# Values' lone product last, PSUM pools swapped by halves, gates from the exponential, and three loads of the setup at other tiles

## The chip, the core and the metric

The kernel runs on one core of one Trainium2 chip. A core has a matmul engine (PE, TensorE), VectorE (DVE), ScalarE (ACT), GpSimd (POOL) and SyncE (SP). SP issues nearly all transfers of this kernel, in the order of the program: an issue that waits holds up all issues behind it. The metric is the device time of one execution in microseconds (us), the median over several runs. The profile is one execution, taken by the hardware profiler; its span runs from the first to the last instruction.

## What is computed

Two attention layers over the same 2048 tokens of width 512, with 32 heads of 16, mixed by a gate per token. Layer A is full softmax attention. Layer B is causal attention inside each of four segments of 512 tokens, plus a memory that is carried from segment to segment. All arithmetic is float32 (matmuls work on sums of two fp32r parts, so one product of two float32 matrices is three products of parts).

```python
g = _sigmoid((x * gate_w).sum(-1, keepdims=True))
a = _A_ref(x, A_wqkv, A_wo)                    # full attention
b = _B_ref(x, B_wq, B_wk, B_wv, B_wo, B_beta)  # four segments, with memory
return g * a + (1 - g) * b
# inside B, per segment:
    g = _sigmoid(beta); num = phi(q) @ M; den = phi(q) @ z + 1e-6
    o = g * (num / den) + (1.0 - g) * a_dot
    M = M + phi(k).T @ v;  z = z + phi(k).sum()
```

## The kernel before, in words

The kernel has two parts. In the **main part** (from about 289 us to the end) PE computes scores and weighted values, ACT the exponentials, DVE the row maxima. The change has no instruction there. In the **setup** (the first 289 us) the projections are made, and everything is stored to DRAM scratch (`qdB`, `kdB`, `kdA`, `vdA`, `vdB`), from where the main part loads it.

The setup is written out in *slots* of twelve matmuls of 512 columns, counted in `now[0]`. Each slot has four *places*, one after each three matmuls, and a function that is posted to (slot, place) issues its instructions there (`post` counts from the present slot, `post_at` is absolute). So each engine's order is fixed by these numbers. The stretches that matter:

- Slots 0 to 21: values and queries of the first half of the tokens. Slots 22 to 35: keys of A.
- **Slots 36 to 49: `v_pair` for the second half of the tokens**, called twice, for row blocks 0, 1 and then 2, 3. Each call makes seven products (a Strassen-like scheme, `ORDER`), one slot each: p1, p2, p7, p6, p5, p3, p4. Two sums X and Y per block live in PSUM: p1, p6, p5 and p3 add to X, whose partial results ACT copies out (`copy_x`); p2 is a Y of its own ("the lone product"), and p7 starts a second Y that p4 ends. DVE adds a copied X and a Y into the values `vs` after p2 (L548), p5 (L553) and p4 (L557). PSUM pools `pr`, `me` and `sm` have 2, 2 and 4 banks; a tile of a pool waits until the tile that had its bank is read. X is taken from `pr`, Y from `me`, in both calls.
- **Slots 50 to 81 (S0 = 50), called tiles 0 to 31 below**: for each of four token chunks c, four query tiles (8c to 8c+3) and four key tiles (8c+4 to 8c+7) of layer B, by `qk_tile`. A tile's PSUM result is copied by ACT (`full`, L426), rounded by ACT to its high part (`q1`, L427), its low part is made by DVE (`q2`, L434), and SP stores both (L423). `q1` and `q2` have three buffers each, so a tile needs the stores of the tile three before. For most tiles POOL makes min(x, 0) (`mn`), ACT its exponential (`ex`, one buffer, L440) and DVE phi (`ph`, L445). At tiles 13, 21 and 29 `mem_q` multiplies by the memory (`num`, `den`) and stores `numd` and `dend` to DRAM; `mem_k` transposes phi(k) (`tps`) and adds to the memory (`mps`), with values loaded back from `vdB` (`load_vB`).
- Beside these, row maxima for layer A (`some_max`, PE L242 into a `sm` bank, DVE reduction L275) run four at a time from slot 39 on.
- **Loads of the setup**: `staged` loads a weight or an x chunk (1 MB in four transfers) and splits it into two parts at given slots; `load_gate` loads four row blocks of x (1 MB) at tiles 2, 8, 16 and 21, and three and four tiles later DVE multiplies them by `gate_w` and sums (`gate_logit`, L781) into `glog`. The product goes to a scratch tile `jk` with the tag `dn`, a single buffer that it shares with the `dn` tile of `mem_q`. `load_vB` loads 2 x 544 KB at tiles 1, 11 and 19.
- **The gates**: `betas` (slot 29) makes sigmoid(beta); `gates` (tile 28) transposes `glog`, takes the sigmoid on ACT, and stores g and 1 - g through POOL. ACT holds one set of function tables at a time: Sigmoid and Exp here are in different ones, so each of them is preceded by an ACT_TABLE_LOAD where the other was last. `gates` ends with an Exp of one number that brings the exponential's tables back.

Of the kernel before, what the change touches and what calls it, by code (L numbers as in the profile page):

```python
# [10 lines left out]
F32 = mybir.dt.float32  # L11
F32R = mybir.dt.float32r
AF = mybir.ActivationFunctionType
ALU = mybir.AluOpType
# [5 lines left out]
D = 512  # L20
# [27 lines left out]
def gated_mix(ctx, tc, x, xT, wqkv, a_wo, b_wq, b_wk, b_wv, b_wo, beta, gate_w, out):  # L48
# [284 lines left out]
    with ExitStack() as p0:  # L333
# [180 lines left out]
                    post(0, 1 + 2 * g, lambda p=p, g=g: done(p, g))  # L514
                slot(prods, not first)

        def v_pair(xo, cs, bs, fill=None, tags=("full", "full", "am", "am")):
# [24 lines left out]

            def done(p, b):
                n = bs.index(b)
                if p == "p1":
                    t["1", b] = copy_x(b, tags[n])
                elif p == "p2":
                    to_vs(p, b, lambda o: V.tensor_add(o, view(Y[b]), view(t["1", b])))  # L548
                elif p == "p6":
                    t["a", b] = copy_x(b, ("q1", "q1", "q1", "q2")[n] if len(bs) == 4 else "am")  # L550
                elif p == "p5":
                    t["5", b] = copy_x(b, tags[n])
# [5 lines left out]
            xbanks = [sm_bank] * 4 if len(bs) == 4 else [pr_bank] * 2  # L558
            ybanks = [pr_bank, pr_bank, me_bank, me_bank] if len(bs) == 4 else [me_bank] * 2
            for p, x, w in ORDER:  # L560
                x, w = xo[x], vops[w]
                if fill and p == "p7":
                    fill()
                prods = []
                for b, xb, yb in zip(bs, xbanks, ybanks):
                    if p == "p1":
                        X[b] = xb()
                    elif p in ("p2", "p7"):
                        Y[b] = yb()
                first = p in ("p1", "p2", "p7")  # L570
                outer = fill and p in ("p1", "p2")
                order = [(b, 0, a, c) for a, c in ((0, 0), (0, 1), (1, 0)) for b in bs] + \
                    [(b, 1, a, c) for b in bs for a, c in PARTS] if outer else \
                    [(b, k, a, c) for b in bs for k in range(2) for a, c in PARTS]
                left = {b: 6 for b in bs}
                for i in range(0, len(order), 12):
                    part = order[i:i + 12]
                    prods = []
                    for m, (b, k, a, c) in enumerate(part):
                        ps = X[b] if p in ("p1", "p6", "p5", "p3") else Y[b]  # L580
                        left[b] -= 1
                        prods.append((ps, x[a][k][:, b * 128:(b + 1) * 128], w[c][k], first and left[b] == 5, left[b] == 0))
                        if left[b] == 0:
                            post(0, m // 3, lambda p=p, b=b: done(p, b))
                    slot(prods, not first)
# [134 lines left out]
        def staged(src, to, key, raws_, homes, load, splits, eng):  # L720

            r = []

            def load_():
                r.extend(raws_())
                load4(src, r)

            def split_(k):
                if k == 0:
                    to[key] = [h if isinstance(h, list) else unit4(h) for h in homes]  # L730
                split(to[key][0][k], to[key][1][k], r[k], eng)
            post_at(*load, load_)
            for k in range(KT):
                post_at(*splits[k], lambda k=k: split_(k))

        def at_u(i):
            return lambda: unit4(i, F32)
# [5 lines left out]
        staged(b_wk, wB, "k", at_u(4), (9, 5), (45, 0), [(48 + k, 3) for k in range(KT)], P)  # L743
        staged(xchunk(1), xcs, 1, at_u(8), (6, 10), (47, 0), [(53 + k, 2) for k in range(KT)], V)
        staged(xchunk(2), xcs, 2, at_u(2), (3, 4), (S0 + 4, 0), [(S0 + 9 + k, 2) for k in range(KT)], V)
        staged(xchunk(3), xcs, 3, at_u(2), (10, 8), (S0 + 14, 0), [(S0 + 18 + k, 2) for k in range(KT)], V)
        vB = {}

        def load_vB(c):
            vB[c] = [vp.tile([128, NG, 2, 4, 17], F32, tag="vs", name="vs") for _ in range(2)]  # L750
            for i, t in enumerate(vB[c]):
                nc.sync.dma_start(t.rearrange("p g b h e -> p g (b h e)"),
                                  vdB[c][:, :, 2 * i:2 * i + 2].rearrange("p g b e -> p g (b e)"))
        for c, n in ((0, 1), (1, 11), (2, 19)):
            post_at(S0 + n, 1, lambda c=c: load_vB(c))

        gw = {}
# [12 lines left out]
                    raw(t)[64 * r + 48:64 * r + 50], ones.unsqueeze(1).broadcast_to([2, 2, CH])))  # L770

        def betas():
            nc.scalar.activation(gh, gh, AF.Sigmoid)
            nc.vector.tensor_scalar(ogh, gh, -1.0, 1.0, op0=ALU.mult, op1=ALU.add)
            for o in range(NO):
                nc.vector.tensor_scalar_mul(gmask[:, o], bmask, gh[:, o:o + 1])
        post_at(29, 0, betas)

        def gate_logit(xg, col):
            jk = wk1.tile([128, D], F32, tag="dn", name="jk")  # L780
            nc.vector.scalar_tensor_tensor(jk, xg, 1.0, gw[0], op0=ALU.mult, op1=ALU.mult,  # L781
                                           accum_out=glog[:, col:col + 1])

        def load_gate(c):
            t = unit4((3, 7, 6, 6)[c], F32)
            for b in range(4):
                t0 = c * CH + 128 * b
                nc.sync.dma_start(t[b], x[t0:t0 + 128])
            for b in range(4):
                post(3 + b // 2, 1 + 2 * (b % 2), lambda b=b: gate_logit(t[b], 4 * c + b))  # L790
# [95 lines left out]
        for n in range(36, S0):  # L886
# [15 lines left out]
        def gates():  # L902
            gps = me_ps.tile([128, CH], F32, tag="me", name="gps")
            nc.tensor.transpose(gps[:16, :128], glog, identf)
            gt = wk1.tile([128, 4, 128], F32, tag="gw", name="gt")
            nc.scalar.activation(gt[:16, 0], gps[:16, :128], AF.Sigmoid)

            nc.scalar.activation(gt[:1, 2, 0:1], eps[:1], AF.Exp)
            nc.vector.tensor_scalar(gt[:16, 1], gt[:16, 0], -1.0, 1.0, op0=ALU.mult, op1=ALU.add)
            for i in range(2):  # L910
                nc.gpsimd.dma_start(gd[i].rearrange("(b t) -> b t", t=128), gt[:16, i])

        for c in range(NCH):
            post_at(S0 + (2, 8, 16, 21)[c], 2, lambda c=c: load_gate(c))
        post_at(S0 + 28, 0, gates)
        for c in range(NCH):
            for o in range(NO):
                qk_tile(wB["q"], xcs[c], o, qd["B", o, c], pqs.append if c else None)
            for o in range(NO):
                then = (lambda pk, o=o, c=c: beside_max(lambda: mem_k(o, c, pk, vB[c]))) if c + 1 < NCH else None  # L920
                qk_tile(wB["k"], xcs[c], o, kd["B", o, c], then)
# [503 lines left out]
```

## Time and profile before

| what | value |
|---|---|
| median of 3 runs | 1760.22 us (1756.73 to 1760.93) |
| the profiled execution | 1755.57 us, its span 1753.4 us |
| granted TensorE clock, mean | 0.999 |
| DVE, ACT, POOL busy | 1605.4, 1445.7, 695.1 us |
| ACT_TABLE_LOADs in the first 300 us | 5, of 1.28 us each |

How to read it: the profile's page gives busy time by engine. A timeline row gives the start, the duration, the engine, the source line, what is written from what, its shape and count, and in brackets the idle time of the engine before it and what ended that. "SPq" rows are the issues of transfers, not the transfers. A row of stretches gives, for each from:to, its length, PE's busy time with the count of matmuls, the granted clock as a share, the mean busy share of the 16 DMA engines, and what they moved. The source lines are those of the kernel before; in the changed one those behind `gate_logit` are one higher.

### The profile page before, as it was taken

How to read it: one execution, taken by the hardware profiler on the slowest of the kernel's cores; microseconds unless marked ns; L12 is line 12 of the kernel's file. 1: busy time of each engine (PE TensorE's matmuls, PEld its weight loads, DVE VectorE, ACT ScalarE, POOL GpSimd, SP SyncE). 2: the span in 40 equal slices, each digit the busy share in tenths (PEclk: the TensorE clock that was granted, in tenths of full speed). 3: DMA queues.
4: the chain of work that ended last, by engine and by line, in shares of the span. 5: the costliest groups of instructions: out<-in, count | busy, mean ns of one | idle time of the engine just before them, and what ended most of it. 6: DMA issues, size and time to landing. Idle time of an engine off the chain costs nothing.

```text
span 1753.4 us, 41543 instructions
## 1 busy us (share of the span) xinstructions
PE 1736.4 (99%) x15157; PEld 878.6 (50%) x15157; DVE 1605.4 (92%) x3371; ACT 1445.7 (82%) x2779; POOL 695.1 (40%) x944
## 2 busy tenths in 40 slices
PE   9999999999999999999999999999999999999998
PEld 7876665444444444444444444444444444444444
DVE  7767867999999999999999999999999999999931
ACT  6543657889898898888898888889889889889884
POOL 1011434324262518353435353444444353535443
PEclk9999999999999999999999999999999999999999
DMA  7677876434454446454545454444444444544542
GB/s 247 197 252 208 286 254 204 120 97 145 119 146 110 136 135 184 127 151 122 142 136 142 130 142 134 135 136 130 148 120 147 127 138 116 152 120 144 149 154 62
DMA packets 167987, 264.96 MB, mean 151 GB/s; under 512 B 38936, under 2 KB 79928, under 8 KB 167784
## 3 DMA queue, kind: packets, MB, share of 16 engines
q1 hardware_dynamic: 166840, 261.07, 50.3%
q8 instruction: 120, 1.97, 0.5%
q0 software_dynamic: 800, 0.97, 0.3%
q14 instruction: 83, 0.68, 0.1%
q10 hardware_dynamic: 144, 0.26, 0.1%
HBM read 177.74 MB, written 83.25 MB: 149 GB/s over the span
## 4 chain that ended last, share of the span: by engine, by line
PE 93%; DVE 3%; DMA 2%; ACT 1%; issue 1%; SPq 0%; DVEq 0%; ACTq 0%
PE ops L155 40%; PE st L1061 27%; PE sm L242 14%; PE pr L385 7%; PE pair L385 2%; PE sm L155 2%; DVE pm L275 1%; DMA qdB<-q 1%; DMA u<-xT 0%; DVE u L403 0%; DVE ph L445 0%; DVE q L434 0%; PE mt_ps L232 0%; PE sm L1061 0%; DVE jk L781 0%
## 5 line engine op out<-in xcount | busy, mean ns | idle before, releaser
L1084 ACT ACTIVATE p<-st 128x512 f32<-128x512 f32 x2261 | 1191.6, 601 | 145.9 <-PE sm L242 93.6
L275 DVE TENSOR_REDUCE pm<-sm 128x1 f32<-128x512 f32 x2048 | 1279.4, 690 | 13.8 <-PE sm L242 13.1
L242 PE MATMUL sm<-kA,qA 48*128 48x512 f32 x2048 | 663.7, 424 | 0.5
L1061 PE MATMUL st<-qA,kA 50*128 50x512 f32 x2014 | 656.7, 432 | 0.0
L155 PE MATMUL ops<-p,vA 128*17 128x256 f32 (+3 forms) x6360 | 552.2, 445 | 0.0
L1061 PEld LDWEIGHTS st<-qA,kA 50*128 50x128 f32 x2014 | 326.8, 185 | 423.5 <-ACT p L1084 380.4
L242 PEld LDWEIGHTS sm<-kA,qA 48*128 48x128 f32 x2048 | 338.4, 185 | 13.0 <-issue 4.2
L1185 POOL TENSOR_TENSOR rcp<-rec,minus 128x32 f32<-128x32 f32 x43 | 234.9, 5463 | 80.8 <-DMA rec<-dend 76.0
L290 DVE CUSTOM_DVE_ANT_0 rest<-sm,mask 128x128 f32<-128x128 f32 (+3 forms) x512 | 249.7, 488 | 0.0
L155 PEld LDWEIGHTS ops<-p,vA 128*17 128x17 f32 x6360 | 129.2, 96 | 214.7 <-issue 183.6
L1065 POOL TENSOR_SCALAR_AFFINE_SELECT p<-p 128x512 f32<-128x512 f32 x128 | 79.8, 640 | 266.5 <-ACT p L1084 262.1
L242 PE MATMUL sm<-kB,qB 48*128 48x128 f32 (+3 forms) x512 | 166.1, 384 | 0.0
L385 PE MATMUL pr<-u,u 128*128 128x512 f32 x392 | 103.4, 403 | 6.1 <-ACT full L426 5.0
L1061 PE MATMUL st<-qB,kB 50*128 50x512 f32 (+1 forms) x495 | 105.4, 329 | 0.3 <-ACT mt L235 0.3
L1061 PEld LDWEIGHTS st<-qB,kB 50*128 50x128 f32 x495 | 68.6, 186 | 62.3 <-ACT p L1084 50.4
L155 PE MATMUL ops<-p,vB 128*17 128x128 f32 (+3 forms) x1504 | 88.3, 350 | 0.2 <-ACT part L1275 0.2
L385 PEld LDWEIGHTS pr<-u,u 128*128 128x128 f32 x392 | 72.7, 191 | 27.2 <-ACT full L426 6.6
L242 PEld LDWEIGHTS sm<-kB,qB 48*128 48x128 f32 x512 | 79.9, 184 | 0.0
L214 POOL TENSOR_TENSOR dm<-pm 128x32 f32<-128x32 f32 x32 | 7.9, 246 | 166.5 <-DVE pm L275 166.5
L431 POOL TENSOR_SCALAR mn<-full 128x512 f32<-128x512 f32 x24 | 37.8, 1577 | 71.2 <-ACT full L426 71.2
L223 POOL CAST ms<-pm 128x16 fp32r<-128x16 f32 x32 | 6.3, 198 | 127.2 <-DVE pm L290 127.1
L1201 POOL TENSOR_TENSOR v<-v,inv 128x512 f32<-128x512 f32 x31 | 39.9, 1286 | 29.3 <-DMA inv<-rdA 22.2
(224 smaller groups left out, 1419.3 us busy)
## 6 DMA issues: line engine op xcount, KB each, us to landing
kA<-kdA SPq DMA_DIRECT2D x256, 128.0 KB
vA<-vdA SPq DMA_DIRECT2D x31, 544.0 KB
kA<-kdA SPq DMA_DIRECT2D x256, 64.0 KB
qB<-qdB SPq DMA_DIRECT2D x192, 64.0 KB
kB<-kdB SPq DMA_DIRECT2D x192, 64.0 KB
kdA<-q SPq DMA_DIRECT2D x32, 256.0 KB
qA<-qdA SPq DMA_DIRECT2D x64, 128.0 KB
qdB<-q SPq DMA_DIRECT2D x32, 256.0 KB
```

Of the source, the lines that this page charges most:

```text
L155: behind[0] = nc.tensor.matmul(*args, **kw)
L214: nc.gpsimd.tensor_sub(dm, pm[:, :, :, 2:4], pm[:, :, :, 0:2])
L242: nc.tensor.matmul(ps[:, n0:n0 + n], rows(qt[u][:, :, s * 128:(s + 1) * 128], h, 48), rows(k[:, :, k0:k0 + n], h, 48), start=True, stop=True)
L275: nc.vector.tensor_reduce(pm[:, h, s, kc:kc + 1], ps, axis=AX.X, op=ALU.max, negate=True)
L290: nc.vector.tensor_tensor_reduce(out=tri["rest"][:, 0:w], in0=ps[:, n0:n0 + w], in1=tri["mask"][:, CH - w:], scale=-1.0, scalar=3.0e38, op ...
L385: nc.tensor.matmul(ps, l, r, start=start, stop=stop, skip_group_check=chained)
L431: nc.gpsimd.tensor_scalar_min(ph["mn"], full, 0.0)
L1061: nc.tensor.matmul(ps[:, n0:n0 + CH - q0], rows(k[:, :, b * 128:(b + 1) * 128], h, 50), rows(q[:, :, q0:], h, 50), start=True, stop=True)
L1065: nc.gpsimd.affine_select(out=x, in_=x, pattern=[[0, 4], [1, 128]], base=0, channel_multiplier=-1, compare_op=ALU.is_ge, fill=0.0)
L1084: nc.scalar.activation(p[:, h], ps, AF.Exp, scale=SCALE)
L1185: eng.tensor_tensor(r, rec, minus, op=ALU.pow)
L1201: eng.tensor_mul(k["v"], k["v"], k["inv"])
```

## The change

Three parts.

1. `v_pair` in slots 36 to 49 makes p2 last (p1, p7, p6, p5, p3, p4, p2). Its Y is taken from the pool of X. The first call has X in `me` and Y in `pr`, the second the reverse. Copies of p6 go to the tag `q1`, those of p5 to `am`. The first two query tiles take their bank from `me`.
2. Both sigmoids become Exp of -x on ACT, then add 1 and reciprocal on DVE; the Exp of one number is gone. `betas` moves from slot 29 to slot 17, `gates` from tile 28, place 0 to tile 25, place 1.
3. `load_gate` runs at tiles 2, 8, 13 and 18, `load_vB` for c = 2 at tile 21, and the last x chunk at tile 15 (its splits at 19 to 22); `gate_logit` writes its product over x itself, so `jk` is gone. The buffers `u0` to `u10` are dealt out anew to suit.

```diff
-            for p, x, w in ORDER:
+            xbanks = [xbank] * 2 if xbank else [sm_bank] * 4
+            ybanks = [ybank] * 2 if ybank else [pr_bank, pr_bank, me_bank, me_bank]
+            for p, x, w in ORDER if fill else ORDER[:1] + ORDER[2:] + ORDER[1:2]:
...
-                        Y[b] = yb()
+                        Y[b] = yb() if fill or p == "p7" else xb()
...
-        staged(xchunk(3), xcs, 3, at_u(2), (10, 8), (S0 + 14, 0), [(S0 + 18 + k, 2) for k in range(KT)], V)
+        staged(xchunk(3), xcs, 3, at_u(2), (9, 5), (S0 + 15, 0), [(S0 + 19 + k, 2) for k in range(KT)], V)
...
-        for c, n in ((0, 1), (1, 11), (2, 19)):
+        for c, n in ((0, 1), (1, 11), (2, 21)):
...
-            nc.scalar.activation(gh, gh, AF.Sigmoid)
+            nc.scalar.activation(gh, gh, AF.Exp, scale=-1.0)
+            nc.vector.tensor_scalar_add(gh, gh, 1.0)
+            nc.vector.reciprocal(gh, gh)
...
-        post_at(29, 0, betas)
+        post_at(17, 0, betas)
...
-            jk = wk1.tile([128, D], F32, tag="dn", name="jk")
-            nc.vector.scalar_tensor_tensor(jk, xg, 1.0, gw[0], op0=ALU.mult, op1=ALU.mult,
+            nc.vector.scalar_tensor_tensor(xg, xg, 1.0, gw[0], op0=ALU.mult, op1=ALU.mult,
...
-            t = unit4((3, 7, 6, 6)[c], F32)
+            t = unit4((4, 7, 5, 3)[c], F32)
...
-        v_pair(xo1, (2, 3), range(2), tags=("full", "full"))
-        v_pair(xo1, (2, 3), range(2, 4), tags=("full", "full"))
+        v_pair(xo1, (2, 3), range(2), xbank=me_bank, ybank=pr_bank)
+        v_pair(xo1, (2, 3), range(2, 4), xbank=pr_bank, ybank=me_bank)
...
-            nc.scalar.activation(gt[:16, 0], gps[:16, :128], AF.Sigmoid)
-
-            nc.scalar.activation(gt[:1, 2, 0:1], eps[:1], AF.Exp)
+            nc.scalar.activation(gt[:16, 0], gps[:16, :128], AF.Exp, scale=-1.0)
+            nc.vector.tensor_scalar_add(gt[:16, 0], gt[:16, 0], 1.0)
+            nc.vector.reciprocal(gt[:16, 0], gt[:16, 0])
...
-            post_at(S0 + (2, 8, 16, 21)[c], 2, lambda c=c: load_gate(c))
-        post_at(S0 + 28, 0, gates)
+            post_at(S0 + (2, 8, 13, 18)[c], 2, lambda c=c: load_gate(c))
+        post_at(S0 + 25, 1, gates)
...
-                qk_tile(wB["q"], xcs[c], o, qd["B", o, c], pqs.append if c else None)
+                qk_tile(wB["q"], xcs[c], o, qd["B", o, c], pqs.append if c else None, bank=me_bank if c == 0 and o < 2 else None)
```

The order on PE at the start of the second `v_pair` call. `u_252` is block 2 of the left operand of p1 and `u_253` that of p2, `u_256` with `qtmp` is p7, and `sm` rows are the maxima. Before:

```order
L242 MATMUL sm<-kA_192,qA_1220 128x512 x4
L385 MATMUL pr<-u_252,u_906 128x512 x12
L242 MATMUL sm<-kA_193,qA_1220 128x512 x4
L385 MATMUL pr<-u_253,u_938 128x512 x12
L242 MATMUL sm<-kA_193,qA_1220 128x512 x4
L385 MATMUL pr<-u_256,qtmp 128x512 x12
```

Now the same place:

```order
L385 MATMUL pr<-u_253,u_946 128x512 x12
L242 MATMUL sm<-kA_192,qA_1222 128x512 x4
L385 MATMUL pr<-u_252,u_914 128x512 x12
L242 MATMUL sm<-kA_193,qA_1222 128x512 x4
L385 MATMUL pr<-u_256,qtmp 128x512 x12
```

p7 no longer follows p2 of its own call: the p2 that stands ahead of p1 here is the last product of the first call.

The order on SP from the stores of tile 18 to those of tile 22 (`qdB` and `kdB` rows are the stores, two per tile; `vs<-vdB` is the load of values, `u<-x` the gate's x, `numd` and `dend` the memory's results). Before:

```order
L174 DMA kB_200<-kdB_92 16x2x512 x6
L423 DMA qdB_111<-q_2589 128x512
L752 DMA vs<-vdB_126 128x8x136 x2
L769 DMA kB_201<-qtmp 2x2x512
L423 DMA qdB_111<-q_2590 128x512
L769 DMA kB_201<-qtmp 2x2x512
L423 DMA qdB_119<-q_2661 128x512
L423 DMA qdB_119<-q_2662 128x512
L423 DMA kdB_96<-q_2697 128x512
L423 DMA kdB_96<-q_2698 128x512
L788 DMA u_2720<-x 128x512 x4
L830 DMA numd_130<-u_2753 128x512 x4
```

Now, from the last store of tile 17 (between the two pieces stand the other rows of `kA` and those of `qB` and `kB`, as before):

```order
L423 DMA qdB_103<-q_2516 128x512
L789 DMA u_2540<-x 128x512 x4
L769 DMA kB_200<-qtmp 2x2x512
L177 DMA kA_198<-kdA_64 32x1024
L177 DMA kA_198<-kdA_64 16x1024
```

```order
L423 DMA qdB_111<-q_2588 128x512
L769 DMA kB_201<-qtmp 2x2x512
L423 DMA qdB_111<-q_2589 128x512
L769 DMA kB_201<-qtmp 2x2x512
L423 DMA qdB_119<-q_2654 128x512
L423 DMA qdB_119<-q_2655 128x512
L423 DMA kdB_96<-q_2686 128x512
L752 DMA vs<-vdB_126 128x8x136 x2
L423 DMA kdB_96<-q_2687 128x512
L831 DMA numd_130<-u_2742 128x512 x4
```

The gate's x moved from behind the stores of tile 20 to ahead of the loads of `kA`, `qB` and `kB`; the values moved from between the stores of tile 18 to between those of tile 20, and `numd` follows them with one store between.

The order on ACT around the gates (`gt` is the gate, `gps` the transposed logits). Before:

```order
L427 CAST q_3014<-full 128x512
L440 ACTIVATE ex<-mn 128x512
L906 ACT_TABLE_LOAD
L906 ACTIVATE gt<-gps 16x128
L908 ACT_TABLE_LOAD
L908 ACTIVATE gt<-eps 1x1
L426 COPY full<-pr 128x512
```

Now:

```order
L427 CAST q_2884<-full 128x512
L907 ACTIVATE gt<-gps 16x128
L849 COPY pt<-tps 128x512
L440 ACTIVATE ex<-mn 128x512
L426 COPY full<-pr 128x512
```

The gate's activation stands three tiles earlier and alone. On ACT's whole list one ACT_TABLE_LOAD is left of five, the one ahead of the first copy.

More of the change, by code (lines that the diff above doesn't have):

```diff
@@ L515, in k_pair, with v_pair @@
                 slot(prods, not first)
-        def v_pair(xo, cs, bs, fill=None, tags=("full", "full", "am", "am")):
+        def v_pair(xo, cs, bs, fill=None, xbank=None, ybank=None):
             X, Y, t, vs = {}, {}, {}, {}
@@ L545, in done @@
                 if p == "p1":
-                    t["1", b] = copy_x(b, tags[n])
+                    t["1", b] = copy_x(b, ("full", "full", "am", "am")[n])
                 elif p == "p2":
@@ L549, in done @@
                 elif p == "p6":
-                    t["a", b] = copy_x(b, ("q1", "q1", "q1", "q2")[n] if len(bs) == 4 else "am")
+                    t["a", b] = copy_x(b, ("q1", "q1", "q1", "q2")[n])
                 elif p == "p5":
-                    t["5", b] = copy_x(b, tags[n])
+                    t["5", b] = copy_x(b, ("full", "full", "am", "am")[n] if fill else "am")
                     to_vs(p, b, lambda o: V.tensor_add(o, view(Y[b]), view(t["5", b])))
@@ L557, in done @@
                     to_vs(p, b, lambda o: V.tensor_add(o, view(Y[b]), view(t["a", b])))
-            xbanks = [sm_bank] * 4 if len(bs) == 4 else [pr_bank] * 2
-            ybanks = [pr_bank, pr_bank, me_bank, me_bank] if len(bs) == 4 else [me_bank] * 2
-            for p, x, w in ORDER:
+            xbanks = [xbank] * 2 if xbank else [sm_bank] * 4
+            ybanks = [ybank] * 2 if ybank else [pr_bank, pr_bank, me_bank, me_bank]
+            for p, x, w in ORDER if fill else ORDER[:1] + ORDER[2:] + ORDER[1:2]:
                 x, w = xo[x], vops[w]
@@ L742, in gated_mix @@
         staged(xchunk(0), xcs, 0, raw_ph, (K4[3], 7), (40, 1), spread(48), V)
-        staged(b_wk, wB, "k", at_u(4), (9, 5), (45, 0), [(48 + k, 3) for k in range(KT)], P)
-        staged(xchunk(1), xcs, 1, at_u(8), (6, 10), (47, 0), [(53 + k, 2) for k in range(KT)], V)
-        staged(xchunk(2), xcs, 2, at_u(2), (3, 4), (S0 + 4, 0), [(S0 + 9 + k, 2) for k in range(KT)], V)
-        staged(xchunk(3), xcs, 3, at_u(2), (10, 8), (S0 + 14, 0), [(S0 + 18 + k, 2) for k in range(KT)], V)
+        staged(b_wk, wB, "k", at_u(4), (10, 8), (45, 0), [(48 + k, 3) for k in range(KT)], P)
+        staged(xchunk(1), xcs, 1, at_u(2), (9, 3), (47, 0), [(53 + k, 2) for k in range(KT)], V)
+        staged(xchunk(2), xcs, 2, at_u(5), (6, 4), (S0 + 4, 0), [(S0 + 9 + k, 2) for k in range(KT)], V)
+        staged(xchunk(3), xcs, 3, at_u(2), (9, 5), (S0 + 15, 0), [(S0 + 19 + k, 2) for k in range(KT)], V)
         vB = {}
```

## The prediction

> **What bounds the kernel now.** I read the page's first two lines, then PE's busy time by stretches, cut where stages of the setup begin.
>
> ```profile
> span 1753.4 us, 41543 instructions
> PE 1736.4 (99%) x15157; PEld 878.6 (50%) x15157; DVE 1605.4 (92%) x3371; ACT 1445.7 (82%) x2779; POOL 695.1 (40%) x944
> ```
>
> ```profile
> 104.00:156.71 52.71, 50.18 (x222) 1.00 0.74 223
> 156.71:210.43 53.72, 52.10 (x378) 1.00 0.86 269
> 210.43:242.05 31.62, 31.62 (x298) 1.00 0.70 224
> 242.05:282.31 40.26, 34.49 (x298) 0.96 0.67 230
> 282.31:1753.40 1471.09, 1466.00 (x13534) 1.00 0.47 135
> ```
>
> PE is busy 99% and sets the end; all its idle time is 17 us. The rows are slots 36 to 49 with some of what precedes them, tiles 0 to 13, 14 to 21, 22 to 29, and the rest. The change has no instruction in the last row, where PE is full, so what the setup gains should reach the end whole. The third and fourth row hold the same work (298 matmuls each, eight tiles), and take 31.62 and 40.26: **the fourth loses 8.64 us**, of which PE shows 5.77 as idle; the rest is slower matmuls.
>
> Next, PE's own rows, in time order, at its waits:
>
> ```profile
> 107.08 5.75 PE L385 MATMUL pr<-u,u 128*128 128x512 f32 x24 [1.10 <-DVE full L500]
> ...
> 140.03 1.63 PE L385 MATMUL pr<-u,qtmp 128*128 128x512 f32 x6 [1.43 <-DVE vs L548]
> ...
> 159.66 1.98 PE L242 MATMUL sm<-kA,qA 48*128 48x512 f32 x4
> ...
> 245.00 0.73 PE L242 MATMUL sm<-kA,qA 48*128 48x512 f32 x4
> ...
> 251.86 2.29 PE L242 MATMUL sm<-kA,qA 48*128 48x512 f32 x4
> ...
> 255.45 4.61 PE L385 MATMUL pr<-u,u 128*128 128x512 f32 x12 [0.48 <-ACT full L426]
> ...
> 262.91 3.00 PE L385 MATMUL pr<-u,u 128*128 128x512 f32 x12 [0.48 <-ACT full L426]
> ...
> 277.26 3.03 PE L385 MATMUL pr<-u,u 128*128 128x512 f32 x12 [2.62 <-ACT full L426]
> ```
>
> Two waits in `v_pair` (1.10 and 1.43). Maxima that take 2.29 in place of 0.73. A tile that takes 4.61 in place of 3.00. And 2.62 at tile 29. What stands behind those of tiles 24 to 29 is on DVE, ACT and SP:
>
> ```profile
> 250.52 0.69 DVE L434 TENSOR_TENSOR q<-full,q 128x512 fp32r<-128x512 f32 x1 [6.07 <-DMA qdB<-q]
> ...
> 260.35 0.69 DVE L781 SCALAR_TENSOR_TENSOR jk<-u,gw 128x512 f32<-128x512 f32 x1 [5.55 <-DMA dend<-dn]
> ```
>
> ```profile
> 273.67 1.28 ACT L906 ACT_TABLE_LOAD   x1
> 274.96 0.27 ACT L906 ACTIVATE gt<-gps 16x128 f32<-16x128 f32 x1
> 275.25 1.28 ACT L908 ACT_TABLE_LOAD   x1
> ...
> 276.65 0.56 ACT L426 COPY full<-pr 128x512 f32<-128x512 f32 x1
> ```
>
> ```profile
> 224.64 2.02 SPq L788 DMA_DIRECT2D u<-x  x4
> ...
> 233.34 2.87 SPq L177 DMA_DIRECT2D kA<-kdA  x4
> ...
> 241.90 0.36 SPq L423 DMA_DIRECT2D qdB<-q  x1
> 242.31 1.35 SPq L752 DMA_DIRECT2D vs<-vdB  x2
> 243.70 0.69 SPq L769 DMA_DIRECT2D kB<-qtmp  x1
> 244.49 0.33 SPq L423 DMA_DIRECT2D qdB<-q  x1
> ...
> 249.79 1.76 SPq L788 DMA_DIRECT2D u<-x  x4
> 251.66 2.71 SPq L830 DMA_DIRECT2D numd<-u  x4
> ```
>
> SP runs some 10 us behind. It issues the loads of kA, qB and kB from 233.34 to 241.9. So the second store of tile 18 goes out only at 244.49, behind 1.1 MB of values. Tile 21's low part needs its buffer, and DVE stands for 6.07. Then x and `numd` follow at once, `dend` behind them, and `jk`, sharing a buffer with `dn`, stands for 5.55. Bytes moved in the 20 us before 242, and in the 20 us behind:
>
> ```profile
> DMA packets 2362, 4.13 MB, mean 207 GB/s; under 512 B 436, under 2 KB 468, under 8 KB 2358
> ...
> DMA packets 4987, 6.33 MB, mean 316 GB/s; under 512 B 404, under 2 KB 2452, under 8 KB 4985
> ```
>
> **Part 1, values.** With X of the first call in `me`, p1 no longer waits for DVE's last add of the keys (in `pr`): 1.10 goes. p7 now takes it one product (2.7 us) later, after those adds have ended. In the second call p7 wants a Y bank one product after the first call's p2, no longer straight behind its own p2, whose add ends late:
>
> ```profile
> 139.21 0.68 DVE L548 TENSOR_TENSOR vs<-pr,vt 128x512 f32<-128x512 f32 x1
> ...
> 157.34 1.36 DVE L403 TENSOR_TENSOR u<-ph,kA 128x512 fp32r<-128x512 f32 x1
> 158.62 2.47 DVE L275 TENSOR_REDUCE pm<-sm 128x1 f32<-128x512 f32 x4
> ```
>
> So 1.43 goes too. What is late next is DVE: the splits of the x chunk (0.6 to 1.36 each) stand in slots 48 and 49, and the maxima at 159.66 already wait 1.98 - 0.73 = 1.25 for it. A slot is 3.6 us (3.00 and 0.73, which overlap a little); DVE has 2.47 of maxima, 0.6 per add or split. Slots 47 to 49 now ask 3.7, 3.7, 4.9 = 1.5 too much; with p2 last, slots 48 and 49 ask 4.9 each, 2.6 too much. The wait may grow by up to 1.1; I take 0.6. **Values: -1.10 - 1.43 + 0.6 = -1.9** (bounds -2.5 and -1.4).
>
> **Part 2, gates.** Two table loads and two activations keep ACT from 273.67 to 276.65, 2.98 us, and PE waits 2.62 for the copy behind them. With Exp alone one activation of 0.27 stays, at a tile where ACT waits anyway. DVE gets an add and a reciprocal. The nearest row of a reciprocal is
>
> ```profile
> 1736.58 0.35 DVE L1181 RECIPROCAL rec<-rec 128x32 f32<-128x32 f32 x1 [4.30 <-DMA rec<-odA]
> ```
>
> 0.35 for 32 columns; 128 columns lie between that and four times it, 1.4. I take 0.8, hidden by PE's two banks per pool; uncovered, it costs that. POOL's store of the gates holds up `mn` of the next tile about as long. `betas` moves eight small operations (some 1 us of DVE) to slot 17, where DVE runs without a gap up to this row:
>
> ```profile
> 70.97 0.43 DVE L403 TENSOR_TENSOR kA<-u,kA 128x256 fp32r<-128x256 f32 x1 [2.00 <-ACT kA L402]
> ```
>
> The 2.00 of slack takes them; without it, 1 us. The other two table loads lie where PE does not wait: nothing. The Trainium skill (ScalarE: Activation LUTs, "What ACT_TABLE_LOAD costs") adds a drain of 1.38 us to each switch; by it the gates would give back 2.8 us more, but the activation at 274.96 begins where the load ends, so the rows show no drain.
>
> **Part 3, loads.** The gate's x goes out before the kA block, in the stretch of 207 GB/s, and takes the SP time that the load at 224.64 (2.02) leaves free; so the stores of tile 18 go out at about 243 to 244, as now, but with nothing large ahead. I take 2 us to land (the slot of 6.07 minus 1.1 MB at 316 GB/s, 3.5, gives 2.6), so DVE's 6.07 shrinks to about 2, which two banks of `pr` absorb. The 5.55 of `jk` cannot recur: there is no `jk`, and x has landed. What is late next: values and `numd`, 2.1 MB, now stand together ahead of tile 21's stores, 6.7 us at 316 GB/s, from about 246 to 253. Tile 24 wants those buffers at about 253. I leave 1.0 of PE's loss for it. **Tiles 22 to 29: -8.64 + 1.0 = -7.6**, gates included (bounds -8.6, and -1.7 below).
>
> In tiles 12 to 17 SP issues as many loads as now, x at 13 and the chunk at 15 for the chunk at 14 and x at 16. But the chunk now stands ahead of tile 14's stores. DVE has gaps there that take up some of a delay, such as this one:
>
> ```profile
> 227.13 0.69 DVE L445 SCALAR_TENSOR_TENSOR ph<-full,ex 128x512 f32<-128x512 f32 x1 [1.16 <-ACT ex L440]
> ```
>
> I take **+0.5** (0 to 6.0, what such a queue costs now at tiles 22 to 27: 8.64 - 2.62).
>
> Sum: -1.9 - 7.6 + 0.5 = **-9.0**. Against the profiled execution, 1755.57 (span 1753.4 and 2.2 around it), that is 1746.6. The median of the runs shown is 1760.22, 4.6 above it, and I forecast on its scale: 1751.
>
> **Rivals.**
> - *The wait stays where it is.* Values and `numd` together delay the stores as values and x do now, and tiles 22 to 27 keep their 6.0. For it: the same bytes go in the same 20 us but for 1 MB. Against: nothing waits for `dend`. Then the gates alone give 2.62, less 1.0 that the next `num` products wait when PE comes early: -1.6. With values -1.9: -3.5, 1756.7. Chance 0.20.
> - *The queue moves to tiles 14 to 17.* Half of 6.0 arises there: -9.0 + 2.5 = -6.5, 1753.7. Chance 0.12.
> - *Slower:* the same mechanism at full price in both places. The chunk ahead of tile 14's stores costs 6.0 and tiles 22 to 27 keep 6.0: -3.5 + 6.0 = +2.5, 1762.7. It decides when stores cost PE more than 6.0 + 3.5 = 9.5 us in tiles 12 to 27. Against: the third row has no idle PE now. Chance 0.05.
> - *DVE bounds slots 46 to 50*, so that the bank swap does not do what it says and the values give nothing: -7.1, 1753.1. Chance 0.08.
> - *The half clock stays.* These rows bear on it:
>
> ```profile
> 252.10:255.50 3.40, 2.42 (x9) 1.00 1.04 348
> 255.50:258.90 3.40, 3.40 (x9) 0.53 0.99 379
> ...
> 272.60:276.00 3.40, 2.04 (x9) 1.00 0.28 102
> ```
>
>   The 4.61 (1.6 more than 3.00) is the granted clock at half for one stretch, behind 3.4 us with PE at 71%. At 272.6 PE is at 60% and keeps its clock. If the fall does not hang on the wait, it stays: -7.4, 1752.8. The Trainium skill (TensorE: Matmul & The Clock Gate, "What's actually happening") lets the clock fall after an idle window of about 3.4 us; the length agrees with the 3.4 us at 0.53, but no such idle stretch precedes it here, and by that rule the wait would not be its cause. I keep the wait as cause. Chance 0.08.
>
> **How the numbers follow.** The forecast has the rest, 0.47. About 0.3% (5.3 us) is what a measurement can tell from no change. Faster by more: the forecast, the half clock, DVE and most of the moved queue, 0.71. Slower by more: 0.03, the slower rival beyond its price. Same: 0.26. The range: at best all of 8.6 and 2.5 go (-11.1, 1749), and the runs shown reach 3.5 below their median: 1745. Above, the first rival gives 1756.7 and two of three runs lie within 0.7 of 1760: 1759.
>
> **What would show it.** Right: p1 at slot 36 and p7 at slot 45 without a wait; `gate_logit` never waiting for `dend`; no table load behind the first; the stretch of tiles 22 to 29 near 32.6 us, at full clock. Wrong: DVE waits of several us for `qdB` or `kdB` stores at tiles 16 to 27, maxima of slot 50 above 2.6 us, or a main part that is longer by what the setup gains.

## The result, and the profile after

| kernel | median, us | runs | ratio to the kernel before, 95% interval |
|---|---|---|---|
| changed kernel | 1745.63 (1744.79 to 1747.14) | 4 | 0.9924, 0.9907 to 0.9942 |
| the same on a second chip | 1746.47 (1745.55 to 1748.38) | 4 | 0.9932, 0.9916 to 0.9947 |

The kernel before had 1759.38 beside the first row and 1758.14 beside the second, so the change is worth 13.75 and 11.7 us. The forecast, 1751.0, was 9.2 below the median it started from; the range (1745 to 1759) holds the result at its low end. The two profiled executions differ by less, 1755.57 against 1745.41, since the profiled run of before was among its fastest (24 runs of it on a third chip went from 1754.4 to 1759.3). Stage lengths below are from the profiled pair, in which the span shrank by 9.7.

The page's head after the change:

```profile
span 1743.7 us, 41524 instructions
...
PE 1732.8 (99%) x15157; PEld 878.0 (50%) x15157; DVE 1606.5 (92%) x3375; ACT 1439.4 (83%) x2774; POOL 694.2 (40%) x944
```

PE's busy time by stretches, from the second on cut at the same products as before (slots 36 to 49 with some of what precedes them, tiles 0 to 13, 14 to 21, 22 to 29, the rest); the columns are length, PE busy, granted clock, DMA share, GB/s:

```profile
102.79:154.56 51.77, 51.57 (x227) 1.00 0.74 222
154.56:207.22 52.66, 51.58 (x377) 1.00 0.87 281
207.22:237.85 30.63, 30.63 (x299) 1.00 0.74 251
237.85:272.43 34.58, 32.16 (x297) 0.95 0.78 267
272.43:1743.70 1471.27, 1466.22 (x13534) 1.00 0.46 135
```

The first row starts at another point than before and can't be compared: from the start of the last product of slot 35 (103.11 before, 102.95 now) to tile 0 PE took 53.60 before and takes 51.61 now, 1.99 less for the same 226 matmuls. Tile 0 starts 2.15 earlier (154.56 for 156.71). Tiles 0 to 13 take 1.06 less, 14 to 21 take 0.99 less, 22 to 29 take 5.68 less, and the rest is as long as it was (1471.27 for 1471.09): what the setup gained reached the end. PE's idle time is 10.9 in place of 17.0. The row of 22 to 29 still has 2.4 of idle and a clock of 0.95.

PE's own rows at the places that the prediction named:

```profile
105.67 2.88 PE L385 MATMUL pr<-u,u 128*128 128x512 f32 x12
...
131.76 3.02 PE L385 MATMUL pr<-u,qtmp 128*128 128x512 f32 x12
...
152.78 1.85 PE L242 MATMUL sm<-kA,qA 48*128 48x512 f32 x4
...
157.50 1.93 PE L242 MATMUL sm<-kA,qA 48*128 48x512 f32 x4
...
235.76 1.14 PE L819 MATMUL num<-ph,mbd 32*32 32x512 f32 x32
...
247.34 4.42 PE L385 MATMUL pr<-u,u 128*128 128x512 f32 x12 [2.42 <-ACT full L426]
...
264.69 5.73 PE L385 MATMUL pr<-u,u 128*128 128x512 f32 x24
```

The first two rows are p1 and p7, which had waited 1.10 and 1.43 and now do not. The maxima of slots 49 and 50 take 1.85 and 1.93 where 0.73 is their own time: they now wait 1.12 and 1.20 for DVE. `num` of tile 21 takes 1.14. Tile 24 waits 2.42 and then runs one product at half clock (4.42 for 3.0). From there to the end of tile 29 nothing waits; the last row covers the place of the old 2.62.

What stands behind the 2.42 is on ACT, and behind that on SP (whose rows are issues):

```profile
244.57 0.62 ACT L427 CAST q<-full 128x512 fp32r<-128x512 f32 x1 [4.45 <-DMA qdB<-q]
...
256.33 0.26 ACT L907 ACTIVATE gt<-gps 16x128 f32<-16x128 f32 x1
```

```profile
233.82 4.39 SPq L174 DMA_DIRECT2D qB<-qdB  x6
238.25 2.75 SPq L174 DMA_DIRECT2D kB<-kdB  x6
241.11 0.36 SPq L423 DMA_DIRECT2D qdB<-q  x1
241.52 0.63 SPq L769 DMA_DIRECT2D kB<-qtmp  x1
242.25 0.67 SPq L423 DMA_DIRECT2D qdB<-q  x1
...
245.08 1.35 SPq L752 DMA_DIRECT2D vs<-vdB  x2
```

The first store of tile 18 goes out at 241.11. Before it was 241.90, so SP gained 0.8, while PE reaches tile 22 some 4.2 earlier. ACT writes tile 21's high part into that store's buffer and stands for 4.45. On DVE the store wait comes through ACT; the gates cost a reciprocal of 0.94:

```profile
245.22 0.69 DVE L434 TENSOR_TENSOR q<-full,q 128x512 fp32r<-128x512 f32 x1 [4.85 <-ACT q L427]
...
252.56 0.69 DVE L434 TENSOR_TENSOR q<-full,q 128x512 fp32r<-128x512 f32 x1 [0.99 <-DMA kdB<-q]
...
256.88 0.94 DVE L909 RECIPROCAL gt<-gt 16x128 f32<-16x128 f32 x1
```

### The profile page after: what moved, and what is told of

The parts are those of the page before. It is cut to its first block, busy times and chain, and to the rows that moved or that the text cites. A ratio compares the mean times of both kernels' runs of the same rounds, so it can differ in the third digit from the quotient of the medians.

```text
span 1743.7 us, 41524 instructions
## 1 busy us (share of the span) xinstructions
PE 1732.8 (99%) x15157; PEld 878.0 (50%) x15157; DVE 1606.5 (92%) x3375; ACT 1439.4 (83%) x2774; POOL 694.2 (40%) x944
## 4 chain that ended last, share of the span: by engine, by line
PE 94%; DVE 2%; DMA 1%; ACT 1%; issue 1%; SPq 0%; DVEq 0%; ACTq 0%
PE ops L155 40%; PE st L1062 28%; PE sm L242 14%; PE pr L385 8%; PE pair L385 2%; PE sm L155 2%; DVE pm L275 1%; DMA qdB<-q 1%; DMA u<-xT 0%; PE mt_ps L232 0%; DMA u<-x 0%; DVE u L403 0%; PE sm L1062 0%; DVE q L434 0%; DVE ph L445 0%
```

## Experiments

Stage lengths are differences between the starts of the same products in each profile; medians are of the timed runs. One profile is one execution: two of the changed kernel have 34.58 and 36.56 for tiles 22 to 29, so less than about 2 us there is not read from a single pair. Kernels listed together ran on one chip and share the runs of the kernel before.

### The three parts alone, and the old gates in the new order

The kernel before had 1757.12 here (19 runs, 1755.10 to 1759.23).

**Values alone** (part 1 of the diff, with the buffers that it needs):

```diff
-        v_pair(xo1, (2, 3), range(2), tags=("full", "full"))
+        v_pair(xo1, (2, 3), range(2), xbank=me_bank, ybank=pr_bank)
...
```

> The kernel before with part 1 alone (values; u buffers dealt out as in the change, loads, gates and jk as before). Theory A, the parts add: p1 at slot 36 and p7 at slot 45 have no wait (1.10 and 1.43 gone), DVE gives back some at slots 49 and 50, tile 1 starts about 2.2 us earlier than 161.56, tiles 22 to 29 keep 40.3 us, and the median is 2 us below that of before. Theory B, the store queue sets tiles 22 to 29: SP issues no earlier, so PE that comes 2.2 us earlier waits that much longer there; tiles 22 to 29 take 41.5 us or more and the median is within 1 us of before.

1753.97, ratio 0.9982 (0.9972 to 0.9992): -3.15. Tile 0 starts at 154.41 in place of 156.71. But tiles 22 to 29 grew from 40.26 to 42.31 in this profile: PE came earlier and DVE waited longer for the same transfers, as its waits between 235 and 284 show (total, times, longest):

```profile
DVE q L434 <- DMA qdB<-q: 7.2, 1, 7.2
DVE jk L781 <- DMA dend<-dn: 6.5, 1, 6.5
```

Both had been shorter (6.07 and 5.55). So in this profile, whose span is only 1.2 below that of before, part of the gain is handed back where a queue sets the pace, as theory B has it; the medians, 3.15 apart, do not show it and side with theory A.

**Gates alone** (Exp, add and reciprocal, at the old slot and tile; `betas` likewise):

```diff
...
-            nc.scalar.activation(gt[:16, 0], gps[:16, :128], AF.Sigmoid)
-
-            nc.scalar.activation(gt[:1, 2, 0:1], eps[:1], AF.Exp)
+            nc.scalar.activation(gt[:16, 0], gps[:16, :128], AF.Exp, scale=-1.0)
+            nc.vector.tensor_scalar_add(gt[:16, 0], gt[:16, 0], 1.0)
+            nc.vector.reciprocal(gt[:16, 0], gt[:16, 0])
```

> The kernel before with part 2's functions alone (Exp and reciprocal, no table loads, at the old slot 29 and tile 28). Theory A: the 2.62 us at tile 29 goes, about 1.0 of it comes back as a wait of the num products; and the table load at tile 5 was behind the 1.06 us that tiles 0 to 13 became shorter with the whole change (53.72 to 52.66), so that shows here too: in all -2.7 us. Theory B: the load at tile 5 was hidden behind DVE, tiles 0 to 13 keep 53.7 us, and the 1.06 came with something else: in all -1.6 us.

1755.17, 0.9987 (0.9978 to 0.9996): -1.95. Tiles 0 to 13 took 53.22 (-0.5), tiles 22 to 29 39.15 (-1.1): the 2.62 is gone, and `num` of tile 29 waits 0.99. Theory B's -1.6 is the nearer.

**Loads alone** (part 3, the product over x among it):

```diff
-            jk = wk1.tile([128, D], F32, tag="dn", name="jk")
-            nc.vector.scalar_tensor_tensor(jk, xg, 1.0, gw[0], op0=ALU.mult, op1=ALU.mult,
+            nc.vector.scalar_tensor_tensor(xg, xg, 1.0, gw[0], op0=ALU.mult, op1=ALU.mult,
...
-            post_at(S0 + (2, 8, 16, 21)[c], 2, lambda c=c: load_gate(c))
+            post_at(S0 + (2, 8, 13, 18)[c], 2, lambda c=c: load_gate(c))
...
```

> The kernel before with part 3 alone (loads at the new tiles, product over x, u buffers as in the change; values and gates as before). Theory A: tiles 14 to 21 lose the 1.0 us that num waits at tile 21 (31.6 to 30.6), tiles 22 to 29 go from 40.3 to about 37 us (the gates' 2.6 stays, a wait for the stores of tile 18 stays), in all about -4.5 us. Theory B, bytes and not order set the wait: tiles 22 to 29 keep 39 us or more, in all -1.5 us or less.

1751.09, 0.9962 (0.9948 to 0.9977): -6.0. Tiles 14 to 21 took 30.61 (-1.0), tiles 22 to 29 36.07 (-4.2). The three ratios multiply to 0.9931, as the whole has on the second chip (0.9932): the parts add, within the intervals.

**The changed kernel with sigmoids again**, at slot 17 and tile 25:

```diff
...
-            nc.scalar.activation(gt[:16, 0], gps[:16, :128], AF.Exp, scale=-1.0)
-            nc.vector.tensor_scalar_add(gt[:16, 0], gt[:16, 0], 1.0)
-            nc.vector.reciprocal(gt[:16, 0], gt[:16, 0])
+            nc.scalar.activation(gt[:16, 0], gps[:16, :128], AF.Sigmoid)
+
+            nc.scalar.activation(gt[:1, 2, 0:1], eps[:1], AF.Exp)
```

> The changed kernel with both sigmoids by the Sigmoid table again, at the changed kernel's slots (17 and tile 25), so that four table loads come back. Theory A (table loads cost PE): tiles 0 to 13 go from 52.7 to 53.7 us and tiles 22 to 29 from 34.6 to 37 us, in all +3.5 us over the changed kernel. Theory B (hidden where ACT waits anyway): tiles 0 to 13 stay, tiles 22 to 29 gain under 1 us, in all +1 us or less.

1750.13, 0.9957 (0.9942 to 0.9972), by the ratios 4.4 to 5.8 above the changed kernel (0.9932 and 0.9924). Tiles 22 to 29 took 38.85 for 34.58 and 36.56. ACT's rows, then PE's, at tile 25:

```profile
257.93 0.62 ACT L427 CAST q<-full 128x512 fp32r<-128x512 f32 x1 [2.38 <-DMA kdB<-q]
258.57 1.28 ACT L905 ACT_TABLE_LOAD   x1
259.86 0.27 ACT L905 ACTIVATE gt<-gps 16x128 f32<-16x128 f32 x1
260.14 1.28 ACT L907 ACT_TABLE_LOAD   x1
```

```profile
260.18 0.81 PE L845 MATMUL tps<-identf,ph 128*128 128x128 f32 x4 [3.48 <-ACT gt L905]
260.63 4.54 PE L385 MATMUL pr<-u,u 128*128 128x512 f32 x12
```

The loads stand behind a copy that a store held up, PE waits 3.48, and half clock follows. The new place of the gates is cheap only because the loads are gone, and it is not free: the next transposes need a bank that `gt` must read first, and `gt` stands behind the same copy. PE waits 1.35 for it in the changed kernel's profile on the second chip, and 0 in the first.

### What is left at tile 24, and DVE at slots 48 to 50

Here the changed kernel itself ran beside the three, 1746.47; the kernel before had 1758.14.

> The changed kernel once more, beside the next three on one chip. Expected: -11 to -14 against the kernel before (it was 13.75 below it on another chip, where the kernel before stood 2.3 higher). Tiles 22 to 29 again near 34.6 with a wait of some 2.4 at tile 24 and one stretch of half clock.

0.9932 (0.9916 to 0.9947). Tiles 22 to 29 took 36.56, not the 34.6 expected: the wait at tile 24 was 2.92, again followed by half clock, and `gt` cost 1.35. SP issued the first store of tile 18 only at 242.77, later than in the kernel before (241.90), though PE reached tile 22 at 238.58 for 242.05.

**The small rows on POOL's queue**, twenty transfers of 2 rows each, which had cost SP 0.63 us of issue a piece (the row at 241.52 above is one):

```diff
-                post_at((S0 - 10 if i < 4 else S0 + 10) + i, 1 + 2 * r, lambda t=t, r=r: nc.sync.dma_start(
+                post_at((S0 - 10 if i < 4 else S0 + 10) + i, 1 + 2 * r, lambda t=t, r=r: nc.gpsimd.dma_start(
```

> The changed kernel with the twenty small rows kA/kB<-qtmp (L769) issued by POOL's queue in place of SP's. Theory 'SP lags': what is left at tile 24 is SP's own issue (these rows take 0.6 to 0.7 us each in front of the stores of tile 18); the first store of tile 18 goes out earlier, ACT's wait of 4.45 for it and PE's 2.42 with the half clock behind it go: tiles 22 to 29 near 31.6 in place of 34.6, -3 us against the changed kernel. Rival 'bytes': the store waits for the traffic of values, x and numd, so it lands no earlier: tiles 22 to 29 stay at 34 or more, no change. Second rival: POOL's mn or its splits come late behind the issues, and tiles 0 to 21 grow by what tiles 22 to 29 gain.

1742.73, 0.9909 (0.9894 to 0.9924), 3.7 under the changed kernel, and the two kernels' runs do not overlap. Tiles 22 to 29 took 31.13, tiles 0 to 13 and 14 to 21 were as long as in the changed kernel (52.76 and 30.61). SP's rows, then PE's at tile 24:

```profile
236.14 2.75 SPq L174 DMA_DIRECT2D kB<-kdB  x6
238.99 1.83 SPq L423 DMA_DIRECT2D qdB<-q  x4
```

```profile
245.17 3.01 PE L385 MATMUL pr<-u,u 128*128 128x512 f32 x12
```

All four stores go out from 238.99 on, the wait is gone, and the clock is 1.0 throughout. So what was left was SP's own issue, not the bytes. The first store goes out 2.1 us earlier than in the first profile of the changed kernel and 3.8 earlier than in the one on this chip, and it was enough. PE still waits 0.67 for `gt`.

**The splits of x chunk 0 earlier**:

```diff
-        staged(xchunk(0), xcs, 0, raw_ph, (K4[3], 7), (40, 1), spread(48), V)
+        staged(xchunk(0), xcs, 0, raw_ph, (K4[3], 7), (40, 1), [(44, 0), (45, 0), (47, 0), (47, 2)], V)
```

> The changed kernel with the four splits of x chunk 0 on DVE at slots 44, 45, 47 and 47 in place of four places spread over slots 48 and 49. Theory 'DVE is late at slots 48 to 50' (the +0.6 of the prediction): the maxima's waits of 1.12 and 1.20 at slots 49 and 50 go, slots 36 to 50 shorten by 1 to 2.3 us. As DVE's stores at tile 21 are bound by SP, part of this may come back as a longer wait at tile 24: in the end -0.5 to -2.3. Rival: the adds of the values at slots 44 to 47 become late instead and PE waits for them: no change.

1742.86, 0.9909 (0.9891 to 0.9926), 3.6 under the changed kernel. PE's maxima of slots 49 and 50, and tile 24:

```profile
152.74 0.73 PE L242 MATMUL sm<-kA,qA 48*128 48x512 f32 x4
...
156.35 0.73 PE L242 MATMUL sm<-kA,qA 48*128 48x512 f32 x4
...
244.41 3.01 PE L385 MATMUL pr<-u,u 128*128 128x512 f32 x12 [2.19 <-ACT full L426]
```

Both waits (2.3 us together) are gone, so they were DVE's splits. The gain was larger than expected: the wait at tile 24 (2.19) did not grow, and no half clock followed it.

**Both**:

> Both edits, the small rows on POOL's queue and the earlier splits. If both theories hold the gains add, since the earlier arrival at tile 24 no longer meets a late store: -4 to -5 against the changed kernel, near 1741. If SP's lag is not the cause of what is left at tile 24: no better than the earlier splits alone.

1739.97 (1739.74 to 1740.68), 0.9894 (0.9879 to 0.9909): the best of the study, 6.5 under the changed kernel where 4 to 5 had been expected. Between slot 36 and tile 29 PE then waits three times, 1.0 us in all:

```profile
PE tps L847 <- ACT gt L907: 0.5, 1, 0.5
PE num L819 <- DVE ph L445: 0.3, 1, 0.3
PE pr L385 <- ACT full L426: 0.2, 1, 0.2
```

### What in the loads did it

The kernel before had 1756.79 here (24 runs).

**Only the product over x**, in the kernel before:

```diff
-            jk = wk1.tile([128, D], F32, tag="dn", name="jk")
-            nc.vector.scalar_tensor_tensor(jk, xg, 1.0, gw[0], op0=ALU.mult, op1=ALU.mult,
+            nc.vector.scalar_tensor_tensor(xg, xg, 1.0, gw[0], op0=ALU.mult, op1=ALU.mult,
```

> The kernel before with only the gate's product written over x, without the buffer jk shared with dn. Prediction's step 'the 5.55 of jk cannot recur': DVE's wait of 5.55 at tile 25 goes. If it is what set tile 26's wait (0.48 and the maxima before it), tiles 22 to 29 lose about 1 us; if x itself lands only then (x is issued at 249.79, behind numd by 0), the wait is named after x in place of dend and nothing is gained. Expected: 0 to -1 us.

1751.81, 0.9968 (0.9956 to 0.9979): -5.0, five times the largest gain expected. Tiles 22 to 29 took 36.53 in place of 40.26, though DVE's wait for the store of tile 18 is as long as ever:

```profile
251.43 0.69 DVE L434 TENSOR_TENSOR q<-full,q 128x512 fp32r<-128x512 f32 x1 [6.36 <-DMA qdB<-q]
...
255.63 0.69 DVE L780 SCALAR_TENSOR_TENSOR u<-u,gw 128x512 f32<-128x512 f32 x1
```

x had landed by then; only the buffer shared with `dn` had held the product up.

**The changed kernel with `jk` in the buffer of `dn` again** (the same lines the other way round):

> The changed kernel with jk in the buffer of dn again. With x loaded at tile 18, the products stand at tiles 21 and 22, ahead of or beside dn of tile 21. Theory 'the loads did it': the products no longer meet a store of dend, no wait and no change (within 0.5 us). Rival 'the shared buffer costs in any order': dn waits for jk or jk for dend by some us, and tiles 22 to 29 grow by 2 or more over the changed kernel's 34.6 to 36.6.

1754.51, 0.9990 (0.9980 to 0.9999): nearly all of the change's gain is lost. The rival holds. DVE, and PE behind it:

```profile
257.71 0.69 DVE L783 SCALAR_TENSOR_TENSOR jk<-u,gw 128x512 f32<-128x512 f32 x1 [8.35 <-DMA dend<-dn]
```

```profile
259.16 1.09 PE L848 MATMUL tps<-identf,ph 128*128 128x128 f32 x4 [8.09 <-DVE ph L445]
```

Three of the four products stand ahead of `dn`, the fourth behind it, and it waits 8.35 for the stores of `dend`. PE stands 8.09, since the product is in DVE's order ahead of the `ph` that PE's transposes need.

**Only the values moved**, in the kernel before:

```diff
-        for c, n in ((0, 1), (1, 11), (2, 19)):
+        for c, n in ((0, 1), (1, 11), (2, 21)):
```

> The kernel before with only the load of values for c = 2 moved from tile 19 to tile 21. Theory 'bytes ahead of the store': the second store of tile 18 no longer stands behind values, DVE's 6.07 shrinks to 2 or 3; tiles 22 to 27 gain 2 to 4 us, unless jk's wait for dend grows, since values, x and numd now stand together. Theory 'SP lags': the values cost SP 1.35 of issue only, the wait shrinks by about that much, to 4.5: -1 us or nothing.

1756.86, 0.9998 (0.9989 to 1.0007): nothing. The 6.07 is gone, and `jk` waits longer by as much:

```profile
243.91 0.69 DVE L434 TENSOR_TENSOR q<-full,q 128x512 fp32r<-128x512 f32 x1 [0.44 <-ACT q L427]
...
259.91 0.69 DVE L781 SCALAR_TENSOR_TENSOR jk<-u,gw 128x512 f32<-128x512 f32 x1 [11.65 <-DMA dend<-dn]
```

The tail of the queue, `dend`, goes out at 254.75 for 255.85 while tile 22 starts 1.0 earlier: against the tiles it came no earlier, and `jk` waited for the tail.

**Only the small rows moved** to POOL's queue, in the kernel before (the edit of the small rows above):

> The kernel before with only the twenty small rows kA/kB<-qtmp issued by POOL's queue in place of SP's. Theory 'SP lags': in the kernel before too, the second store of tile 18 went out at 244.49 because SP ran some 10 us behind, so DVE's wait of 6.07 for qdB shrinks by the lag taken away (2 to 3 us) and with it the 4.61 tile of half clock: tiles 22 to 29 from 40.3 to 36 to 37, -3 to -4 us. Rival 'bytes', which the prediction took as cause: the store still stands behind 1.1 MB of values, 3.5 us: the wait stays at 6 and tiles 22 to 29 at 40, no change.

1751.32, 0.9972 (0.9960 to 0.9983): -5.5, where 3 to 4 had been expected. SP, then DVE:

```profile
237.65 0.36 SPq L423 DMA_DIRECT2D qdB<-q  x1
238.05 1.35 SPq L752 DMA_DIRECT2D vs<-vdB  x2
239.50 1.95 SPq L423 DMA_DIRECT2D qdB<-q  x3
```

```profile
245.30 0.69 DVE L434 TENSOR_TENSOR q<-full,q 128x512 fp32r<-128x512 f32 x1 [1.66 <-DMA qdB<-q]
...
255.69 0.69 DVE L781 SCALAR_TENSOR_TENSOR jk<-u,gw 128x512 f32<-128x512 f32 x1 [6.10 <-DMA dend<-dn]
```

The second store still stands behind the values, but goes out at 239.50 in place of 244.49, and the wait falls from 6.07 to 1.66. The values' place in the queue and SP's lag each add to it; taking away either one cures most of that wait.

Put side by side, in order of DVE's waits in these tiles that a transfer ended, straight or through ACT (stores of queries and keys plus `dend`):

| kernel | stores | `dend` | sum | tiles 22 to 29 |
|---|---|---|---|---|
| values alone | 7.17 | 6.50 | 13.7 | 42.31 |
| changed, `jk` back | 5.17 | 8.35 | 13.5 | 43.03 |
| before, values late | 0 | 11.65 | 11.7 | 42.36 |
| before | 6.07 | 5.55 | 11.6 | 40.26 |
| gates alone | 6.10 | 5.34 | 11.4 | 39.15 |
| before, small rows on POOL | 1.66 | 6.10 | 7.8 | 36.39 |
| changed, second chip | 7.52 | 0 | 7.5 | 36.56 |
| changed, sigmoids again | 7.45 | 0 | 7.5 | 38.85 |
| loads alone | 6.75 | 0 | 6.8 | 36.07 |
| before, product over x | 6.36 | 0 | 6.4 | 36.53 |
| changed | 5.84 | 0 | 5.8 | 34.58 |
| changed, splits earlier | 5.37 | 0 | 5.4 | 34.02 |
| changed, small rows on POOL | 2.58 | 0 | 2.6 | 31.13 |
| changed, both edits | 2.40 | 0 | 2.4 | 30.96 |

The length follows the sum (within about 2 us), not either wait by itself: two kernels with a wait of 6 us of one kind (36.39 and 36.53) are 4 us shorter than the one with both. The rows whose gates still load tables at tile 28 hold 1.4 to 2.6 of PE's wait for those besides, and 0.6 and 1.2 of those 4 us are this wait grown shorter (2.62 before, 2.06 and 1.44 in the two). The row with sigmoids again has its 3.48 at tile 25.

## Why the prediction came out right, and where its terms were off

| term, us | predicted | profiled pair | second profile of the changed kernel |
|---|---|---|---|
| values, start of tile 0 | -1.9 | -2.15 | -1.58 |
| tiles 0 to 13 | 0 | -1.06 | -0.88 |
| tiles 14 to 21 | +0.5 | -0.99 | -1.01 |
| tiles 22 to 29 | -7.6 | -5.68 | -3.70 |
| rest | 0 | +0.2 | 0 |
| sum | -9.0 | -9.7 | -7.2 |

That the sum of the pair lies within 0.7 of the forecast is in part luck: the 1.9 that are missing at tiles 22 to 29 are made up by 2.55 in two stages that the prediction had at 0 and +0.5.

**Values: right, by their mechanism.** Both waits went, and DVE became late at slots 49 and 50 as foreseen: 1.12 and 1.20, against 1.25 at one place before, so 1.07 more where I took 0.6 (the bound was 1.1). The early splits show that it was DVE's splits. The term cannot be read to better than about 1 us from one pair: tile 0 starts between 154.46 and 155.13 in four profiles with the new values and gates, and between 155.94 and 158.37 in six with the old values.

**Gates: right.** Alone they gave 1.95, near the 1.6 that the first rival had for them; the reciprocal took 0.94 where I took 0.8. The step "the other two table loads lie where PE does not wait: nothing" was off: tiles 0 to 13 took 52.66 to 52.88 in four profiles with new values and new gates, 53.27 in the changed kernel with sigmoids, 53.22 with the gates alone, and 53.23 to 54.40 in five that had neither. That points to some 0.5 us for the gates there, but it is not shown: with the values alone, and the old gates, it was 53.15, and the five differ by 1.2 among themselves.

**Tiles 14 to 21: the sign was wrong.** I priced a queue that might form behind the chunk. It did not, and `num` of tile 21 fell from 2.1 to 1.14. The loads do this (30.61 with the loads alone, 31.62 with only the product over x). DVE's gate products for the earlier load no longer crowd the end of that stage; this cause is read from DVE's list and was not isolated.

**Tiles 22 to 29: `jk` and the gates right, the stores wrong.** The failed step is "the stores of tile 18 go out at about 243 to 244, as now ... so DVE's 6.07 shrinks to about 2, which two banks of `pr` absorb", and with it "I leave 1.0". The stores went out a little earlier than that, and nothing large stood ahead, but PE came 4.2 earlier while SP's list of issues had shrunk by 0.8 (in the second profile not at all). So the wait was 4.85 and 0.99, 5.84 in all (7.52 in the second profile) and hardly less than the 6.07, of which PE saw 2.42 and a stretch of half clock: about 3.0 left, not 1.0. Waits of several us for stores at these tiles are what the prediction had named as a sign of being wrong; its signs of being right on p1, p7, `dend` and the table loads came, the one on this stretch (near 32.6 at full clock) did not (34.58 at 0.95). SP was treated as a fixed time in place of a queue with its own length. With the small rows off SP the stage takes 31.13, less than the 32.66 that I forecast (40.26 - 7.6).

**Which part of the loads pays was not seen.** "The 5.55 of `jk` cannot recur" was true, but the prediction put the 6.0 of these tiles mainly on the store behind the values (its first rival keeps all of the 6.0 without `jk`). The runs give the larger part of what the change gained to `jk`: its line alone brings 5.0 of the loads' 6.0, moving the values alone nothing, and the whole change with the old line gains only 2.3. The stores' wait alone was partly absorbed, and so was `jk`'s; the two together were not.

**The rivals.** "The wait stays where it is" came half true: ACT's wait for tile 18 stayed, for SP's lag and not for values and `numd`. "The queue moves to tiles 14 to 17" and "slower" did not come. "The half clock stays" came together with a wait, one stretch as before. That the medians gained more (11.7 to 13.75) than the profiled pair lies in the runs of before, whose profiled one stood low among them; the forecast carried the 4.6 between that run and the median over unchanged.

## What to carry to other kernels

A scratch result that nobody reads should not share a buffer with something that is being stored: it waits for the store, and it stands in order ahead of work that others need. When two waits on one engine lie close together, price them as a sum against the slack of the buffers between, and remove each alone before crediting either. And count the issues on a transfer queue as its own work: twenty small transfers of 0.63 us each were worth 3.7 us on another queue, and after a change that makes the compute engine earlier the queue does not become earlier with it.

## What was not expected of the hardware

The granted clock did not follow the length of the wait ahead of it. The loads alone, at tile 24, as PE's row and as the two stretches of 3.41 us on either side of the fall:

```profile
251.44 4.61 PE L385 MATMUL pr<-u,u 128*128 128x512 f32 x12 [2.11 <-ACT full L426]
```

```profile
249.03:252.44 3.41, 1.30 (x7) 0.98 0.88 268
252.44:255.85 3.41, 3.41 (x9) 0.52 1.08 316
```

This product fell to half clock (4.61 for 3.0) after a wait of 2.11, and the changed kernel's after 2.42. The one with the earlier splits kept full clock after 2.19, the one with sigmoids again after 2.66 at tile 24, and the kernel before after 2.62 at tile 29, where the one with only the values moved fell after 2.60. In the stretch ahead of the fall PE was busy 1.30 of 3.41, 38%, so it takes no stretch that is wholly idle. The Trainium skill (TensorE: Matmul & The Clock Gate, "What's actually happening") speaks of an idle window of about 3.4 us and says that the window runs freely: the length agrees, the wholly idle window does not, and a free-running window would explain that of two waits alike only one falls, by where it lies. The traces bear out that the window runs freely: in each of the fourteen, all changes of the granted clock lie a whole number of 3.413 us apart (with the values alone the half clock starts at 252.36 and at 262.60, three times 3.413). Cut on that grid, 2.13 of the changed kernel's wait of 2.42 lie in one stretch, and the 2.19 of the earlier splits lies across the edge of two (1.16 and 1.03), here in this order:

```profile
245.21:248.62 3.41, 1.28 (x6) 1.00 1.01 294
```

```profile
239.97:243.38 3.41, 2.25 (x12) 1.00 0.90 300
243.38:246.79 3.41, 2.38 (x10) 1.00 1.04 299
```

So it matters where a wait lies. Between 100 us and the end of tile 29 the fourteen profiles have eight stretches at full clock with PE busy less than 44%, and half clock followed each of them; above 74% it followed none. Between 45% and 74% it followed five and spared others, so what sets it there stays open, as does the fall at 71% that the prediction showed: in four of the five, that one among them, maxima that wait count as busy (rows like the 2.29 for 0.73). A fall costs about 1.4 to 1.6 us on top of its wait (4.42 and 4.61 less 3.0).
